# Row thresholds on VectorE instead of GpSimd, and new issue times for loads in the ordering, in a thresholded attention with a gated feed-forward

## The chip, the cores and the metric

The kernel runs on one core of one Trainium2 chip. The metric is the device time of an execution in microseconds (us). Before the change it was 568.11 us, the median of 3 runs (567.13 to 568.92). A difference of under one per cent is therefore only read from rounds in which a kernel and the kernel before alternate on the same chip, and the ratios below come with a 95% interval.

## The reference

Shortened:

```python
def _attn_ref(q, k, v, tau):                     # 8 batches, 8 heads, 576 rows, 64 wide
    scores = (1.0 / np.sqrt(64)) * np.matmul(q, k.transpose(0, 1, 3, 2))
    thresh = np.max(scores, axis=-1, keepdims=True) - tau          # tau = 0.02
    scores = np.where(scores >= thresh, scores, -1e9)
    attn = np.exp(scores - np.max(scores, axis=-1, keepdims=True))
    attn = attn / (np.sum(attn, axis=-1, keepdims=True) + 1e-09)
    return np.matmul(attn, v)

def _moe_ref(x, w_gate, w_val, w_out, rms_g):    # 4608 tokens, 512 wide, 1536 hidden
    xn = x / np.sqrt(np.mean(x * x, axis=-1, keepdims=True) + 1e-06) * rms_g
    g = xn @ w_gate
    return ((g * (1 / (1 + np.exp(-g)))) * (xn @ w_val)) @ w_out
```

The attention's output, heads side by side, is the feed-forward's x.

## The kernel before

The attention goes in 144 steps. One step takes two heads and 128 query rows: TensorE makes the scores into two buffers in PSUM, the memory that this kernel's matmuls write (line 566), VectorE copies them negated into SBUF, where its other tiles lie, and makes the row maximum of each head on the way (line 589), a threshold is formed from the two maxima (line 596), and ScalarE, in 64 of the steps with GpSimd, masks and exponentiates. Feed-forward matmuls fill TensorE between the steps. `mx` holds the two negated maxima of a row, `nth` the two thresholds that ScalarE and GpSimd read:

```python
for h in range(2):
    def ttr(o, h=h):
        nc.vector.tensor_tensor_reduce(
            out=ssb[a][:, h], in0=s_ps[h][:, ROW_AT:ROW_AT + S], in1=zrow, scale=-1.0 / 8.0, scalar=3.0e38,
            op0=ALU.add, op1=ALU.min, accum_out=mx[m][:, h:h + 1])
    ttr_of[s, h] = add("DVE", COST["ttr"], s - 1, [so, o_c] + exp_of.get(s - NSS, []), ttr)

def nthr(o):
    nc.gpsimd.tensor_scalar(out=nth[m], in0=mx[m], scalar1=tau, scalar2=None, op0=ALU.add)

tn = add("POOL", COST["pool_tiny"], s - 4, [ttr_of[s, 0], ttr_of[s, 1]], nthr)
# ... (the ways "p" on ScalarE alone and "g" with GpSimd; both wait for tn)
def mask(o, h=h):                                             # way "g", 64 times
    nc.gpsimd.tensor_scalar(out=wsb[s % NW][:, h], in0=ssb[a][:, h], scalar1=nth[m][:, h:h + 1],
                            scalar2=None, op0=ALU.is_le)      # 1.73 us
def take(o, h=h, es=es):
    nc.gpsimd.tensor_tensor(out=wsb[s % NW][:, h], in0=wsb[s % NW][:, h], in1=esb[es], op=ALU.mult)  # 1.28 us
```

Nothing is issued in the order of this text. Each `add` describes an operation with an engine, an assumed cost in ns, a priority and what it needs; `order_ops` works out from these one order for all engines when the kernel is built, and each engine's part of that order becomes its sequence of instructions. An assumed cost is thus never executed; it only moves instructions in the queues.

Of the kernel before, what the change touches and what calls it, by code (L numbers as in the profile page):

```python
# [11 lines left out]
ALU = mybir.AluOpType  # L12
# [3 lines left out]
COST = dict(  # L16
    s_main=932.0, s_virt=900.0, tr_qk=530.0, tr4=230.0, tr_full=440.0, av_main=310.0, av_virt=480.0, ffn4=216.0, warm=3500.0,
    ttr=690.0, evac_qk=600.0, evac_half=380.0, evac_kt=350.0, prelu=700.0, exp2=1250.0, exp1=690.0, exp0=690.0,
    mask_d=750.0, mask_g=1740.0, take_g=1300.0, trw=510.0, evac_w=450.0, evac_wp=900.0, rz=180.0, xmul=420.0, sq=800.0, xn=720.0,
    pool_tiny=270.0, pool_mean=800.0, pool_dma=850.0, cast_v=650.0, cast_vt=420.0, cast_w=720.0,  # L20
    sp=480.0, sp_v=650.0, sp_w=600.0, sp_tr=1300.0, sp_qk=900.0, sp_tl=630.0,
)
DMA_NS = dict(qk=1250.0, tl=700.0, v=880.0, vt=350.0, wt=1700.0, xt=800.0, out=800.0, w=820.0, wo=2500.0)
SWITCH = 170.0
# [102 lines left out]
def kernel(  # L127
# [12 lines left out]
    nc = tc.nc  # L140
# [3 lines left out]
    tau = float(tau)  # L144
# [9 lines left out]
    def sb(name, shape, dt=FP32):  # L154
        return konst.tile(shape, dt, tag=name, name=name)
# [28 lines left out]
    mx = [sb(f"mx{i}", [128, 2]) for i in range(6)]  # L184
    nth = [sb(f"nth{i}", [128, 2]) for i in range(6)]
# [30 lines left out]
    def gated(o, step):  # L216
        gates.append((o, step))
        return o

    def add(eng, cost, prio, deps, fn, **kw):  # L220
        o = Op(eng, cost, prio, deps, fn, **kw)
        ops.append(o)
        return o
# [315 lines left out]
    pre = {}  # L539
    ttr_of, exp_of, wt_of, av_of = {}, {}, {}, {}  # L540
# [42 lines left out]
    def emit_softmax(s, so):  # L583

        a = s % NSS
        m = s % 6
# [5 lines that stand above are left out]

            ttr_of[s, h] = add("DVE", COST["ttr"], s - 1, [so, o_c] + exp_of.get(s - NSS, []), ttr)

        def nthr(o):
            nc.gpsimd.tensor_scalar(out=nth[m], in0=mx[m], scalar1=tau, scalar2=None, op0=ALU.add)  # L596

        tn = add("POOL", COST["pool_tiny"], s - 4, [ttr_of[s, 0], ttr_of[s, 1]], nthr)
        wfree = [w_read.get(s - NW)]
        done = []  # L600
        ways = WAYS[s % len(WAYS)] if s >= FIRST else "pp"
        pls = []
        for h in range(2):
            way = ways[h]
            if way == "p":
                def prelu(o, h=h):
                    nc.scalar.activation(out=ssb[a][:, h], in_=ssb[a][:, h], func=PRELU, scale=-1.0,  # L607
                                         bias=nth[m][:, h:h + 1], **PRELU_KW)

                def ex(o, h=h):  # L610
                    nc.scalar.activation(out=wsb[s % NW][:, h], in_=ssb[a][:, h], func=AF.Exp)  # L611

                def ex2(o):
                    nc.scalar.activation(out=wsb[s % NW], in_=ssb[a], func=AF.Exp)  # L614

                pls.append(add("ACT", COST["prelu"], s + 0.5, [tn], prelu))
                if ways != "pp":
                    done.append(add("ACT", COST["exp0"], s + 0.5, pls + wfree, ex))
                elif h:
                    done.append(add("ACT", COST["exp2"], s + 0.5, pls + wfree, ex2))  # L620
            else:
                es = pre.get("n", 0) % NES
                pre["n"] = pre.get("n", 0) + 1

                def ex(o, h=h, es=es):
                    nc.scalar.activation(out=esb[es], in_=ssb[a][:, h], func=AF.Exp, scale=-1.0,  # L626
                                         bias=nth[m][:, h:h + 1])

                e = add("ACT", COST["exp1"], s + 0.4, [tn, pre.get(("es", es))], ex)
                if way == "d":  # L630
                    def mask(o, h=h, es=es):
                        nc.vector.scalar_tensor_tensor(
                            out=wsb[s % NW][:, h], in0=ssb[a][:, h], scalar=nth[m][:, h:h + 1], in1=esb[es],
                            op0=ALU.is_le, op1=ALU.mult)

                    st = add("DVE", COST["mask_d"], s + 0.4, [e] + wfree, mask)
                    done.append(st)
                else:
                    def mask(o, h=h):
                        nc.gpsimd.tensor_scalar(  # L640
                            out=wsb[s % NW][:, h], in0=ssb[a][:, h], scalar1=nth[m][:, h:h + 1], scalar2=None,
                            op0=ALU.is_le)

                    def take(o, h=h, es=es):
                        nc.gpsimd.tensor_tensor(out=wsb[s % NW][:, h], in0=wsb[s % NW][:, h], in1=esb[es],  # L645
                                                op=ALU.mult)

                    mk = add("POOL", COST["mask_g"], s + 0.4, [tn] + wfree, mask)
                    st = add("POOL", COST["take_g"], s + 0.4, [e, mk], take)
                    done.append(mk)  # L650
                pre["es", es] = st
                done.append(st)
        exp_of[s] = done

        if s < N_PE or s < N_ALT and s % 2:
            def tr(o):
                for j in range(9):
                    r, c = divmod(j, 5)
                    nc.tensor.transpose(ring[o.slot[r]].bitcast(FP16)[:, 128 * c:128 * c + 128],  # L659
                                        wsb[s % NW].rearrange("p h s -> p (h s)")[:, 128 * j:128 * j + 128], id16)  # L660

            t = add("PE", COST["trw"], s + 2.4, done + av_of.get(s - NWT, []), tr, ring="R", nring=2)
            w_read[s] = t
            w_ready[s] = []
            for r, (lo, hi) in enumerate(((0, 5), (5, 9))):
                def ev(o, r=r, lo=lo, hi=hi):
                    eng = nc.gpsimd if W_EVAC[r] == "POOL" else nc.vector
                    eng.tensor_copy(out=wt[s % NWT][:, lo:hi], in_=ring[t.slot[r]].bitcast(FP16)[
                        :, 0:128 * (hi - lo)].rearrange("p (c n) -> p c n", n=128))

                w_ready[s].append(add(W_EVAC[r], COST["evac_w" if W_EVAC[r] == "DVE" else "evac_wp"], s + 2.4, [t], ev, frees=(t, r)))
        else:
            def tdma(o):
                nc.sync.dma_start_transpose(out=wt[s % NWT], in_=wsb[s % NW].rearrange("p h s -> p (h s)"))

            t = add("SP", COST["sp_tr"], s, done + av_of.get(s - NWT, []), tdma, dma=DMA_NS['wt'])
            w_read[s] = t
            w_ready[s] = [t]
# [90 lines left out]
    def emit_ffn(slot, parts, ready_step, pace, streamed):  # L769
# [55 lines left out]
        if streamed:  # L825

            acc = None
            for fc, (hi, m_) in enumerate(hs):
# [7 lines left out]
                if not acc:  # L836

                    acc, mo.pick = mo, ACC
                outs.append(mo)
# [69 lines left out]
    for c in range(DFF // 512):  # L909
        for d in range(0, 4, 2):  # L910
            for w_dram, w_sb in ((moe_w_gate, wg), (moe_w_val, wv)):
# [7 lines left out]
                lo = gated(add("SP", COST["sp_w"], pr, w_use[slot], load, dma=2 * DMA_NS['w'], bulk=True), pr)  # L919
# [13 lines left out]
    for j in range(4):  # L933
        o = add("POOL", COST["pool_dma"], W_FROM + W_STEP * n + j + WO_AT, [], lambda o, j=j: nc.gpsimd.dma_start(
            out=wo[:, 3 * j:3 * j + 3], in_=wo_src[:, 3 * j:3 * j + 3]), dma=DMA_NS['wo'], bulk=True)
# [3 lines left out]
    for s, (ci, p) in enumerate(steps):  # L939
        kind, b, c = chunks[ci]  # L940
        so = s_of[s] = emit_s(s)
        emit_softmax(s, so)
        if p % 2:
            emit_av(s)
        if p == NP - 1:
            gi, j = place[ci]
            xt_op[ci] = emit_x(ci, s, gi % NXT, 128 * j)
            if ci in last_of:
                g = groups[last_of[ci]]
                emit_ffn(last_of[ci] % NXT, [(ci_of[x], xt_op[ci_of[x]]) for x in g], s + (ELAG if place[ci][0] < NELAG else LAG), PACE,  # L950
                         last_of[ci] >= len(groups) - STREAMED)
            for bb in ([b] if kind == "m" else [2 * b, 2 * b + 1]):
                left[bb] -= 1
                if not left[bb] and bb + 2 < B:
                    emit_batch_inputs(bb + 2)
# [12 lines left out]


PACE = 13.0  # L970
ACC = (4, 6)
OPENS = ((4,), (6,))
NHF = 12
# [69 lines left out]
```

## Time and profile before

| | before |
|---|---|
| median time | 568.11 us |
| span of the profiled execution | 568.3 us |
| TensorE busy | 558.4 us, 98% |
| VectorE busy | 427.2 us, 75% |
| ScalarE busy | 457.4 us, 80% |
| GpSimd busy | 322.4 us, 57% |

TensorE is the bound (98% busy, and 89% of the chain that ended last), so time on another engine counts only where it makes TensorE stand still. The average hides when that can happen. The page's second part gives the busy tenths of each engine in 40 slices of 14.2 us; three of its lines from the kernel before:

```profile
DVE  4899977969958588758895789659875886586354
ACT  4999899999878787979898898778978897884332
POOL 2378946976747457666766658555666555551000
```

VectorE is over 80% busy in the slices from about 14 to 71 us, and ScalarE until about 140. Whatever is added to VectorE has the least room there.

### The profile page before, as it was taken

The page shows a single profiled execution, that of the slowest core. Times are in us where ns is not written, and L with a number is a line of the kernel's source. Part 1 is how long each engine was busy: PE and PEld are TensorE (multiplying, and loading weights), DVE is VectorE, ACT ScalarE, POOL GpSimd, SP SyncE. Part 2 cuts the span into 40 slices and gives each one's busy share as a digit, 9 for nine tenths or more (in the row PEclk, how much of TensorE's full clock was granted, in tenths as well). Part 3 has the DMA queues.
Part 4 walks back from the last instruction along what each step waited for, and adds up shares of the span by engine and source line. Part 5 has one row for each costly group of instructions (what it writes and reads, how often), then busy time and mean ns, then how long its engine had stood idle before and what let it go on. Part 6 is the DMA issues. An engine that isn't in the chain of part 4 may idle for free.

```text
span 568.3 us, 13686 instructions
## 1 busy us (share of the span) xinstructions
PE 558.4 (98%) x5000; PEld 334.7 (59%) x5000; DVE 427.2 (75%) x1093; ACT 457.4 (80%) x739; POOL 322.4 (57%) x462
## 2 busy tenths in 40 slices
PE   8999999999999999999999999999999999999997
PEld 4666766767676555555555555545555455454674
DVE  4899977969958588758895789659875886586354
ACT  4999899999878787979898898778978897884332
POOL 2378946976747457666766658555666555551000
PEclk9999999999999999999999999999999999999999
DMA  8999998769994686999876799789887565633211
GB/s 187 250 289 282 178 195 184 161 132 202 167 202 104 136 159 149 177 177 187 178 160 148 142 186 181 161 168 162 174 167 184 88 96 86 178 81 44 84 37 38
DMA packets 270019, 88.98 MB, mean 157 GB/s; under 512 B 252544, under 2 KB 262272, under 8 KB 269952
## 3 DMA queue, kind: packets, MB, share of 16 engines
q1 hardware_dynamic: 267168, 86.02, 74.1%
q0 software_dynamic: 1600, 1.57, 1.8%
q8 instruction: 39, 0.64, 0.5%
q10 hardware_dynamic: 1184, 0.52, 0.3%
q14 instruction: 28, 0.23, 0.1%
HBM read 37.75 MB, written 9.44 MB: 83 GB/s over the span
## 4 chain that ended last, share of the span: by engine, by line
PE 89%; DVE 3%; DMA 2%; issue 2%; ACT 2%; POOL 1%; SPq 0%; DVEq 0%; POOLq 0%; ACTq 0%
PE s_ps L566 28%; PE ring L792 16%; PE ring L797 16%; PE ring L853 14%; PE ring L697 6%; PE ring L303 2%; PE ring L693 2%; DVE ssb L589 2%; DMA qkn<-in_q_dram 1%; PE s_ps L831 1%; PE s_ps L853 1%; PE ring L659 1%; PE s_ps L797 1%; PE ring L364 1%; DMA stage<-in_q_dram 1%
## 5 line engine op out<-in xcount | busy, mean ns | idle before, releaser
L589 DVE CUSTOM_DVE_ANT_0 ssb<-s_ps,zrow 128x576 f32<-128x576 f32 x288 | 207.8, 754 | 67.7 <-PE s_ps L566 60.5
L607 ACT ACTIVATE ssb<-ssb,nth 128x576 f32<-128x576 f32 x224 | 165.9, 766 | 32.4 <-POOL nth L596 32.1
L566 PE MATMUL s_ps<-qkt 64*128 64x288 f32 x1024 | 170.2, 429 | 1.4 <-DVE mx L589 1.1
L566 PEld LDWEIGHTS s_ps<-qkt 64*128 64x128 f32 x1024 | 96.2, 186 | 53.5 <-DVE mx L589 16.2
L640 POOL TENSOR_SCALAR wsb<-ssb,nth 128x576 f16<-128x576 f32 x64 | 110.5, 1726 | 9.7 <-DMA wt<-wsb 2.9
L792 PE MATMUL ring<-xnT,wg 128*128 128x512 f16 (+1 forms) x548 | 112.9, 328 | 0.4 <-DVE sl L809 0.4
L797 PE MATMUL ring<-xnT,wv 128*128 128x256 f16 (+1 forms) x544 | 111.4, 327 | 0.6 <-ACT qTv L472 0.3
L596 POOL TENSOR_SCALAR nth<-mx 128x2 f32<-128x2 f32 x144 | 31.6, 220 | 133.9 <-DVE mx L589 120.6
L809 DVE SCALAR_TENSOR_TENSOR sl<-th,ring 128x512 f32<-128x512 f32 (+1 forms) x137 | 75.9, 554 | 25.9 <-ACT th L806 24.6
L614 ACT ACTIVATE wsb<-ssb 128x1152 f16<-128x1152 f32 x80 | 92.9, 1161 | 1.9
L806 ACT ACTIVATE th<-ring 128x512 f32<-128x512 f32 (+1 forms) x137 | 66.3, 486 | 28.9 <-PE ring L792 26.4
L853 PE MATMUL ring<-wo,hf 128*128 128x512 f16 x384 | 89.3, 380 | 0.0
L645 POOL TENSOR_TENSOR wsb<-wsb,esb 128x576 f16<-128x576 f16 x64 | 81.8, 1278 | 8.8 <-ACT esb L626 4.4
L814 DVE TENSOR_TENSOR hf<-ring,sl 128x256 f16<-128x256 f32 (+1 forms) x136 | 75.9, 558 | 10.0 <-PE s_ps L566 0.5
L797 PEld LDWEIGHTS <-wv 128*128 128x128 f16 x576 | 52.2, 98 | 42.9 <-issue 12.3
L792 PEld LDWEIGHTS <-wg 128*128 128x128 f16 x576 | 52.0, 98 | 41.0 <-issue 11.6
L853 PEld LDWEIGHTS <-hf 128*128 128x128 f16 x408 | 37.4, 98 | 47.2 <-issue 6.6
L626 ACT ACTIVATE esb<-ssb,nth 128x576 f16<-128x576 f32 x64 | 49.2, 768 | 7.1 <-POOL nth L596 7.0
L697 PE MATMUL ring<-va,wt 128*128 128x65 f16 (+1 forms) x1264 | 52.8, 193 | 0.0
L697 PEld LDWEIGHTS <-wt 128*128 128x128 f16 (+1 forms) x1280 | 48.7, 100 | 3.4
L611 ACT ACTIVATE wsb<-ssb 128x576 f16<-128x576 f32 x64 | 43.6, 681 | 1.6
L693 PE MATMUL ring<-va,wt 128*128 128x130 f16 (+1 forms) x158 | 35.1, 227 | 0.1
(68 smaller groups left out, 448.1 us busy)
## 6 DMA issues: line engine op xcount, KB each, us to landing
vst<-in_v_dram SPq DMA_DIRECT2D x32, 256.0 KB, 3.2
qkn<-in_k_dram SPq DMA_DIRECT2D x31, 256.0 KB, 3.8
out_dram<-osb SPq DMA_DIRECT2D x31, 256.0 KB, 2.6
qkn<-in_q_dram SPq DMA_DIRECT2D x28, 256.0 KB, 4.1
stage<-in_moe_w_gate_dram SPq DMA_DIRECT2D x6, 512.0 KB, 6.6
stage<-in_moe_w_val_dram SPq DMA_DIRECT2D x6, 512.0 KB, 6.3
wt<-wsb SPq DMA_TRANSPOSE x128, 3.1
wo<-in_moe_w_out_dram POOLq DMA_DIRECT2D x4, 384.0 KB, 7.6
```

The source lines that it names most:

```text
L566: nc.tensor.matmul(s_ps[h][rows, ROW_AT + n * part:ROW_AT + n * part + n], lhs(hs), kT[i][p][h][hs, n * part:n * part + n], start=True, st ...
L589: nc.vector.tensor_tensor_reduce(out=ssb[a][:, h], in0=s_ps[h][:, ROW_AT:ROW_AT + S], in1=zrow, scale=-1.0 / 8.0, scalar=3.0e38, op0=ALU.a ...
L607: nc.scalar.activation(out=ssb[a][:, h], in_=ssb[a][:, h], func=PRELU, scale=-1.0, bias=nth[m][:, h:h + 1], **PRELU_KW)
L614: nc.scalar.activation(out=wsb[s % NW], in_=ssb[a], func=AF.Exp)
L640: nc.gpsimd.tensor_scalar(out=wsb[s % NW][:, h], in0=ssb[a][:, h], scalar1=nth[m][:, h:h + 1], scalar2=None, op0=ALU.is_le)
L645: nc.gpsimd.tensor_tensor(out=wsb[s % NW][:, h], in0=wsb[s % NW][:, h], in1=esb[es], op=ALU.mult)
L697: nc.tensor.matmul(ring[o.slot[0]][rs, at:at + D + 1], w[:, 5 * h + j, rs], va[vi][:, p, 2 * j + h], start=False, stop=(h == 1 and j == 3))
L792: nc.tensor.matmul(ring[o.slot[0]][:, 0:n], wg[d][:, fs], xnT[slot][:, d, 0:n], start=(d == 0), stop=(d == 3))
L797: nc.tensor.matmul(ring[o.slot[0]][:, 0:n], wv[d][:, fs], xnT[slot][:, d, 0:n], start=(d == 0), stop=(d == 3))
L809: nc.vector.scalar_tensor_tensor(out=sl[i][:, 0:n], in0=th[i][:, 0:n], scalar=1.0, in1=ring[g.slot[0]][:, 0:n], op0=ALU.add, op1=ALU.mult)
L814: nc.vector.tensor_tensor(out=hf[hi][:, 0:n], in0=ring[vv.slot[0]][:, 0:n], in1=sl[i][:, 0:n], op=ALU.mult)
L853: nc.tensor.matmul(ring[(first or o).slot[0]], hf[hs[fc][0]][:, 128 * j:128 * (j + 1)], wo[:, fc], start=(fc == 0), stop=(fc == NFC - 1))
```

## The change: its intent and the diff

The threshold of a step is one tiny addition. On GpSimd it stands in line behind masks of 1.73 us and products of 1.28 us, and ScalarE waits for it, 39.1 us in all. The change gives it to VectorE, directly behind the two maxima that it needs. A second part sets assumed issue times of loads nearer to those of the profile before (there loads of queries and keys on line 293 took 694 and 626 ns in the median, of values 578 ns); that moves instructions in the order and changes none.

```diff
-    sp=480.0, sp_v=650.0, sp_w=600.0, sp_tr=1300.0, sp_qk=900.0, sp_tl=630.0,
+    sp=420.0, sp_v=600.0, sp_w=600.0, sp_tr=1300.0, sp_qk=680.0, sp_tl=630.0,
...
-        def nthr(o):
-            nc.gpsimd.tensor_scalar(out=nth[m], in0=mx[m], scalar1=tau, scalar2=None, op0=ALU.add)
-
-        tn = add("POOL", COST["pool_tiny"], s - 4, [ttr_of[s, 0], ttr_of[s, 1]], nthr)
+        tns = []
+        for lo, hi in ((0, 1), (1, 2)) if NTH == "EACH" else ((0, 2),):
+            def nthr(o, lo=lo, hi=hi):
+                (nc.gpsimd if NTH == "POOL" else nc.vector).tensor_scalar(
+                    out=nth[m][:, lo:hi], in0=mx[m][:, lo:hi], scalar1=tau, scalar2=None, op0=ALU.add)
+
+            tns.append(add("POOL" if NTH == "POOL" else "DVE", COST["pool_tiny"] if NTH == "POOL" else NTHC, s - 4,
+                           [ttr_of[s, h] for h in range(lo, hi)], nthr))
...  (the readers of tn take tns[h % len(tns)])
+NTH = 'DVE'
+NTHC = 80.0
```

`NTH` also allows "POOL" (GpSimd) and "EACH" (one threshold for each head).

More of the change, by code (lines that the diff above doesn't have):

```diff
@@ L614, in ex2 @@
                     nc.scalar.activation(out=wsb[s % NW], in_=ssb[a], func=AF.Exp)
-                pls.append(add("ACT", COST["prelu"], s + 0.5, [tn], prelu))
+                pls.append(add("ACT", COST["prelu"], s + 0.5, [tns[h % len(tns)]], prelu))
                 if ways != "pp":
@@ L627, in ex @@
                                          bias=nth[m][:, h:h + 1])
-                e = add("ACT", COST["exp1"], s + 0.4, [tn, pre.get(("es", es))], ex)
+                e = add("ACT", COST["exp1"], s + 0.4, [tns[h % len(tns)], pre.get(("es", es))], ex)
                 if way == "d":
@@ L646, in take @@
                                                 op=ALU.mult)
-                    mk = add("POOL", COST["mask_g"], s + 0.4, [tn] + wfree, mask)
+                    mk = add("POOL", COST["mask_g"], s + 0.4, [tns[h % len(tns)]] + wfree, mask)
                     st = add("POOL", COST["take_g"], s + 0.4, [e, mk], take)
```

## The prediction

> **What bounds the kernel now**
>
> I read, in this order: the busy shares and the chain of waits on the page, busy time by stretch, the list of who waited for whom, the groups by line and shape, and the order of instructions where TensorE stood still. First the page:
>
> ```profile
> PE 558.4 (98%) x5000; PEld 334.7 (59%) x5000; DVE 427.2 (75%) x1093; ACT 457.4 (80%) x739; POOL 322.4 (57%) x462
> ...
> PE 89%; DVE 3%; DMA 2%; issue 2%; ACT 2%; POOL 1%; SPq 0%; DVEq 0%; POOLq 0%; ACTq 0%
> ```
>
> TensorE is busy 98% of the span and makes up 89% of the chain that ended last. VectorE (75%), ScalarE (80%) and GpSimd (57%) have room on average. An average hides stages, so next comes busy time by stretch (columns: stretch, then busy us and instruction count of PE, weight loads, VectorE, ScalarE, GpSimd; granted clock; DMA share; GB/s):
>
> ```profile
> 0.00:30.00 30.00, 27.10 (x225) 17.67 (x225) 20.82 (x62) 21.56 (x36) 8.73 (x24) 1.00 0.94 226
> 30.00:60.00 30.00, 28.51 (x318) 20.29 (x318) 27.65 (x80) 28.32 (x41) 24.65 (x47) 1.00 1.15 274
> 60.00:120.00 60.00, 59.49 (x659) 41.45 (x657) 50.32 (x142) 53.74 (x95) 43.37 (x58) 1.00 0.90 169
> 120.00:240.00 120.00, 119.00 (x1140) 75.07 (x1137) 93.44 (x246) 102.55 (x173) 73.61 (x101) 1.00 0.83 162
> 240.00:360.00 120.00, 120.00 (x1071) 66.92 (x1070) 93.98 (x231) 105.01 (x163) 77.93 (x108) 1.00 0.86 170
> ...
> 520.00:569.00 49.00, 44.29 (x316) 29.48 (x314) 22.88 (x55) 14.44 (x35) 1.44 (x3) 0.98 0.14 46
> ```
>
> TensorE is idle 2.9 us in the first 30, 1.5 in the next 30, 0.5 up to 120, 1.0 up to 240, nothing from 240 to 520, and 4.0 after 520 (568.3 less 520 less 44.29), which is the last output leaving. That is 9.9 us in all. Some waiting hides inside rows that count as busy: in the chain, a block of eight score matmuls (line 566) takes 1.17 us when its inputs are there and 1.86 to 1.91 us five times before 80 us. Five times 0.7 is 3.5 us more. So about 13 us of TensorE time is not work, and some 8 of them (the first 6.3 us, when the first query tile is awaited, of which part is idle; the store at the end) cannot be touched by row thresholds. What this change can win is bounded by roughly 5 us, 1% of the time, unless the new order packs TensorE better.
>
> Who waits on the thresholds (columns: waiter, what ended the wait, total us, times, longest):
>
> ```profile
> POOL nth L596 <- DVE mx L589: 120.6, 68, 9.3
> ...
> ACT ssb L607 <- POOL nth L596: 32.1, 39, 2.0
> ...
> POOL va L486 <- DMA vst<-in_v_dram: 14.3, 8, 4.3
> ...
> ACT esb L626 <- POOL nth L596: 7.0, 13, 1.8
> ```
>
> GpSimd's own 120.6 us of waiting for the maxima costs nothing by itself. ScalarE's 39.1 us (32.1 + 7.0) of waiting for thresholds is the target. How one such wait reaches TensorE (start us, length, engine and line, what it does, idle time before):
>
> ```profile
> 69.64 0.69 POOL L734 TENSOR_SCALAR xn<-xsb,ir 128x512 f16<-128x512 f32 x1
> ...
> 70.41 0.52 POOL L596 TENSOR_SCALAR nth<-mx 128x2 f32<-128x2 f32 x2
> ...
> 70.67 0.77 ACT L607 ACTIVATE ssb<-ssb,nth 128x576 f32<-128x576 f32 x1 [1.92 <-POOL nth L596]
> ...
> 71.35 0.36 ACT L806 ACTIVATE th<-ring 128x256 f32<-128x256 f32 x1
> ...
> 71.74 0.42 DVE L809 SCALAR_TENSOR_TENSOR sl<-th,ring 128x256 f32<-128x256 f32 x1 [1.68 <-ACT th L806]
> ...
> 72.22 0.38 PE L792 MATMUL ring<-xnT,wg 128*128 128x256 f16 x2 [0.43 <-DVE sl L809]
> ```
>
> GpSimd was in a normalisation (line 734) until about 70.3 us, so two thresholds came late and back to back; ScalarE stood still for 1.92 us; its tanh for the feed-forward came late; VectorE's product waited 1.68 us; TensorE stood 0.43 us for the PSUM buffer that this product frees. The same happens at 172.75 us, where a threshold sits behind a mask and its product, and a TensorE idle of 0.33 us follows at 176.49.
>
> [...]
>
> [...] 384 out-projection matmuls average 380 ns, yet four such 512-column matmuls follow the four before them after 0.87 us (261.53 to 262.40), about 217 ns each. I therefore look at TensorE's gaps and not at its share, and still find few.
>
> [...]
>
> [...]
>
> [...]
>
> **The change part by part**
>
> ```profile
> L640 POOL TENSOR_SCALAR wsb<-ssb,nth 128x576 f16<-128x576 f32 x64 | 110.5, 1726 | 9.7 <-DMA wt<-wsb 2.9
> ...
> L596 POOL TENSOR_SCALAR nth<-mx 128x2 f32<-128x2 f32 x144 | 31.6, 220 | 133.9 <-DVE mx L589 120.6
> ```
> ```profile
> L589 DVE DVE_READ_ACCUMULATOR2_ANT mx<- 128x1 f32 x288 | 23.9, 83 | 0.0
> ...
> L267 DVE MEMSET mhalf<- 128x1 f32 x1 | 0.1, 59 | 0.0
> ```
>
> The first fence is GpSimd's groups (busy us, mean ns of one, idle before); the second VectorE's small instructions by shape.
>
> *Removed from GpSimd:* 144 thresholds of 220 ns, 31.6 us. GpSimd goes from 322 to about 291 us (51%). Off the path, except that masks start earlier.
>
> *Added to VectorE:* 144 thresholds of about 60 ns, 9 us busy: 427 to about 436 us (77%). The slot is longer than its busy time. Today the accumulator read (83 ns) starts together with the next instruction and is hidden (251.08: both). The threshold needs its result, so it must wait it out; and a dependent VectorE instruction starts some 0.04 us after the one it needs (the reciprocal ends at 255.97, its product starts at 256.01). 0.08 + 0.04 + 0.06 = 0.18 us, times 144 is 26 us of VectorE time. It comes after the second maximum, so the score buffers are released as before; what moves back is the next evacuation or product.
>
> *The wait that shrinks:* from the end of the second maximum to ScalarE's start it is 0.33 us at best today (262.59 to 262.92) and 2 us behind a mask. It becomes about 0.16 us, always. Of ScalarE's 39 us I expect some 30 to vanish from this entry. ScalarE's busy time, 457 us, stays.
>
> *What reaches the end:* (a) To 60 us: VectorE is busy 27.65 of 30 us in the second stretch and stands in the chain between score blocks. Of 16 steps I take half to have VectorE last: 8 x 0.18 = +1.4 us. ScalarE waited 1.8 us for thresholds there, in four places; half of it is worth -0.9. Sum +0.5. (b) 60 to 240: the two stalls told above go, each with the stretched score block after it, about 1.0 us each: -2.0; VectorE runs without pause around 140 to 143 us, where two more slots cost +0.3. Sum -1.7. (c) 240 to 520: TensorE has no idle time, so 0 to -0.5; I take -0.3. (d) The end: nothing, since no thresholds are left after 512 us. Together -1.5 us.
>
> *Issue times of loads:* these numbers change no instruction, only the order that is worked out at build time. The trace supports the new ones: query and key loads took 0.61 to 0.71 us to issue (0.68 in place of 0.90), value loads 0.57 to 0.59 (0.60). With them the order will place loads earlier or tighter on the queue; GpSimd waited 14.3 us for value tiles, 4.28 of it just before the 172 us stall. I take -0.5 us, with 3 us either way, because a new order shuffles every engine.
>
> [...] GpSimd is busy about half the time with instructions of up to 1.73 us. If a random half of the thresholds met one and waited half of some 1.2 us, that would be 72 x 0.6 = 43 us of VectorE. But a mask waits for this very threshold, so the next one, about 3.5 us later, mostly finds the 3.0 us of mask and product done. I take a third of it, 15 us of VectorE time, spread where TensorE has other work: net effect about 0.
>
> Sum: 568.1 - 1.5 - 0.5 = 566.1 us. I predict 566 us, ratio 0.996.
>
> **Rivals**
>
> *1. TensorE's order and work decide, the thresholds never mattered.* For it: no TensorE idle time from 240 to 520 us, while ScalarE waited for thresholds there too (most of the 39 us). Against it: the two chains above. It would make 567 to 569 us.
>
> [...] Against it: the ordering just told. If a wait of about 1 us came in a third of the steps, TensorE would run out of free PSUM buffers (four in the ring) in a good many: 20 to 30 stalls of 0.5 us, 578 to 583 us.
>
> *3. The start becomes VectorE-bound.* For it: 92% VectorE in 30 to 60 us. All 16 steps paying 0.18 us, with nothing won by ScalarE, is +3 us: 570 us.
>
> *4. The new order happens to pack better*, with fewer stretched score blocks and loads of the start a microsecond or two earlier: 561 to 563 us.
>
> **Range and chances**
>
> My value lies 2 us below before. The upper side of the range is rival 3 and a mild rival 2, the lower side rival 4: 560.5 to 571.5 us. Faster by over 2% needs under 556.8 us, an 11 us gain, more than the touchable idle time: 0.03. Slower by over 2% needs over 579.5 us, which only a full lock brings, or an order gone wrong: 0.05. Within 2%: 0.92.
>
> **What would show it right or wrong**
>
> Right: the thresholds stand under VectorE, x144 near 60 ns; ScalarE's wait entry for thresholds falls under 12 us; GpSimd falls by 31 us; TensorE's busy time by stretch shows less idle from 60 to 240 us and nothing new elsewhere. The lock: thresholds far over 60 ns, or VectorE idle before them, ended by nothing, while a mask runs. Rival 3: more idle or stretched score blocks before 60 us, released by the maxima. The prediction is wrong if TensorE shows idle time between 240 and 520 us, or if the span moves by over 5 us with TensorE's idle time unchanged[...].

Passages that no trace or run of this case shows are cut from it, and the cuts are marked. The sum came to 568.1 - 1.5 - 0.5 = 566.1 us, with 0 for the paragraph before it. That paragraph is on the lock: a threshold on VectorE that lasts until an instruction on GpSimd ends. The kernel before has no threshold on VectorE, so its trace could not show one. Rival 2 is that such waits come often. The 60 ns of a threshold, and with them the 9 us and the 0.06 us of the slot, are the author's estimate, which no trace showed; the nearest figure of the trace is the memset of one element, 59 ns.

## The result, and the profile after

The changed kernel took 573.11 us (median of 5 runs, 572.07 to 573.58), the kernel before 568.04 us beside it (5 runs). The ratio is 1.0086, interval 1.0068 to 1.0104: slower by 0.9%, outside the predicted range of 560.5 to 571.5 us. Ratios are from the mean times of the fast runs of both kernels in the same rounds, so not quite the ratio of the medians quoted. All runs were with granted clocks of 0.994 to 1.000.

From the page of the changed kernel, the busy line and the engines' shares of the chain that ended last:

```profile
PE 559.7 (98%) x5000; PEld 335.4 (59%) x5000; DVE 457.4 (80%) x1237; ACT 460.8 (81%) x739; POOL 290.7 (51%) x318
...
PE 83%; DVE 11%; ACT 2%; DMA 2%; issue 1%; SPq 0%; DVEq 0%
```

GpSimd fell by 31.7 us as intended. VectorE rose by 30.2 us, over three times the 9 us predicted, and its share of the chain rose from 3% to 11%. By stretch (columns as in the prediction):

```profile
0.00:30.00 30.00, 26.08 (x232) 17.50 (x233) 22.68 (x70) 22.07 (x37) 7.43 (x18) 1.00 0.94 228
30.00:60.00 30.00, 28.31 (x314) 20.09 (x312) 29.22 (x85) 28.63 (x40) 23.74 (x38) 1.00 1.13 270
60.00:120.00 60.00, 58.88 (x627) 40.59 (x624) 53.89 (x155) 52.22 (x91) 36.63 (x38) 1.00 0.93 170
120.00:240.00 120.00, 119.81 (x1136) 75.88 (x1136) 101.54 (x279) 103.13 (x170) 65.75 (x67) 1.00 0.81 158
240.00:360.00 120.00, 120.00 (x1042) 65.17 (x1039) 97.89 (x257) 103.28 (x161) 68.53 (x72) 1.00 0.81 162
...
520.00:571.00 51.00, 46.64 (x327) 30.53 (x324) 24.62 (x58) 15.59 (x36) 1.44 (x3) 1.00 0.13 45
```

From 240 to 520 us TensorE still has no idle time. Before 60 us it is idle for 5.6 us (3.92 + 1.69) where it was 4.4; from 60 to 120 us for 1.12 where it was 0.51; from 120 to 240 us for 0.19 where it was 1.00. So a stall did go, and others came. A second profile of the changed kernel (the control changed_again below) tells which of this is chance: it has 3.41 us of idle time before 60 us, less than the kernel before, but again 0.93 us from 60 to 120 and 0.17 from 120 to 240. Only the growth from 60 to 120 us repeats; VectorE is busy for 53.9 of the 60 us there. (The two profiled spans differ by 2.4 us and the medians by 5: the profiled execution of the kernel before, 570.23 us, was at the slow end of its runs. The profiles tell where, the rounds tell how much.)

Waits on the thresholds, and in the first line GpSimd's wait for value tiles, which was 14.3 us (waiter, what ended the wait, total us, times, longest):

```profile
POOL va L486 <- DMA vst<-in_v_dram: 26.5, 11, 8.3
...
ACT ssb L611 <- DVE nth L598: 19.1, 28, 1.9
...
ACT esb L630 <- DVE nth L598: 14.9, 32, 1.4
```

ScalarE waits 34.0 us for thresholds (19.1 + 14.9) where it waited 39.1 us. The wait that the change was to remove has mostly stayed, now for VectorE.

The threshold itself, in the view of its tile (duration in ns as least/median/greatest, then first and last start) and in the group list (busy us, mean ns, idle before):

```profile
L598 DVE TENSOR_SCALAR nth<-mx x144: 157/170/1079, 10.2 to 511.5; 128x2 f32<-128x2 f32 x144
```

```profile
L598 DVE TENSOR_SCALAR nth<-mx 128x2 f32<-128x2 f32 x144 | 37.5, 260 | 4.9
```

The median is 170 ns, the mean 260 and the greatest 1079. A few very long ones lift the mean. In the order of time, one of them (start us, length, engine, line):

```profile
61.62 1.29 POOL L649 TENSOR_TENSOR wsb<-wsb,esb 128x576 f16<-128x576 f16 x1
61.75 0.08 DVE L589 DVE_READ_ACCUMULATOR2_ANT mx<- 128x1 f32 x1
61.87 1.07 DVE L598 TENSOR_SCALAR nth<-mx 128x2 f32<-128x2 f32 x1
...
62.85 0.81 DVE L672 COPY wt<-ring 128x640 f16<-128x640 f16 x2
...
62.97 1.44 ACT L611 ACTIVATE ssb<-ssb,nth 128x576 f32<-128x576 f32 x2 [1.60 <-DVE nth L598]
...
63.38 0.22 PE L697 MATMUL ring<-va,wt 128*128 128x130 f16 x1 [0.26 <-DVE wt L672]
```

The maximum is there at 61.83 us. The threshold starts at 61.87 and ends at 62.94, 0.03 us after GpSimd's product, which started before it, ends (61.62 + 1.29 = 62.91). Behind it, VectorE's two copies for the transposed weights start late, TensorE waits for those copies at 63.38, and ScalarE has stood still for 1.60 us. In the trace, 39 of 144 thresholds lasted over 0.2 us, and each of them ended 0.02 to 0.03 us after an instruction on GpSimd: products (21), casts of values and weights (12), normalisations (5), a mask (1). I call this the lock; the traces show when such a threshold ends, not what holds it. It is not taken against every instruction on GpSimd: nine thresholds of usual length ran wholly inside one, seven of them inside the one-element power of the normalisation (`ir`), which held none (it lasts about 0.57 us; they started 98 to 346 ns after it and took 169 or 170 ns). The chain of waits names long thresholds too (start us, length, what):

```profile
58.28 0.63 DVE nth L598
...
61.87 1.07 DVE nth L598
```

Around these two lines the chain is on VectorE without a break, from 32 to over 65 us.

### The profile page after: what moved, and what is told of

Same layout as the page of the kernel before. It is cut to its first block, busy times and chain, and to the rows that moved or that the text cites. A ratio compares the mean times of both kernels' runs of the same rounds, so it can differ in the third digit from the quotient of the medians.

```text
span 570.7 us, 13657 instructions
## 1 busy us (share of the span) xinstructions
PE 559.7 (98%) x5000; PEld 335.4 (59%) x5000; DVE 457.4 (80%) x1237; ACT 460.8 (81%) x739; POOL 290.7 (51%) x318
## 4 chain that ended last, share of the span: by engine, by line
PE 83%; DVE 11%; ACT 2%; DMA 2%; issue 1%; SPq 0%; DVEq 0%
PE s_ps L566 25%; PE ring L796 15%; PE ring L857 15%; PE ring L801 14%; PE ring L701 6%; DVE ssb L589 5%; PE ring L303 2%; PE ring L697 2%; DVE nth L598 1%; PE s_ps L801 1%; DVE wt L672 1%; DVE hf L818 1%; DVE sl L813 1%; DMA qkn<-in_q_dram 1%; PE s_ps L835 1%
## 5 line engine op out<-in xcount | busy, mean ns | idle before, releaser
L611 ACT ACTIVATE ssb<-ssb,nth 128x576 f32<-128x576 f32 x224 | 166.0, 767 | 19.8 <-DVE nth L598 19.1
L566 PEld LDWEIGHTS s_ps<-qkt 64*128 64x128 f32 x1024 | 97.4, 186 | 54.0 <-DVE mx L589 14.3
L796 PE MATMUL ring<-xnT,wg 128*128 128x256 f16 (+1 forms) x564 | 114.5, 325 | 0.1
L801 PE MATMUL ring<-xnT,wv 128*128 128x512 f16 (+1 forms) x520 | 108.2, 330 | 0.8 <-DVE xsb L719 0.7
L813 DVE SCALAR_TENSOR_TENSOR sl<-th,ring 128x256 f32<-128x256 f32 (+1 forms) x141 | 76.7, 544 | 19.8 <-ACT th L810 19.3
L810 ACT ACTIVATE th<-ring 128x256 f32<-128x256 f32 (+1 forms) x141 | 67.6, 481 | 28.9 <-PE ring L796 22.2
L818 DVE TENSOR_TENSOR hf<-ring,sl 128x512 f16<-128x512 f32 (+1 forms) x130 | 73.6, 566 | 10.4 <-PE ring L801 0.9
L630 ACT ACTIVATE esb<-ssb,nth 128x576 f16<-128x576 f32 x64 | 49.5, 773 | 15.1 <-DVE nth L598 14.9
L598 DVE TENSOR_SCALAR nth<-mx 128x2 f32<-128x2 f32 x144 | 37.5, 260 | 4.9
```

Of the source, the lines that this page charges most:

```text
L566: nc.tensor.matmul(s_ps[h][rows, ROW_AT + n * part:ROW_AT + n * part + n], lhs(hs), kT[i][p][h][hs, n * part:n * part + n], start=True, st ...
L611: nc.scalar.activation(out=ssb[a][:, h], in_=ssb[a][:, h], func=PRELU, scale=-1.0, bias=nth[m][:, h:h + 1], **PRELU_KW)
L796: nc.tensor.matmul(ring[o.slot[0]][:, 0:n], wg[d][:, fs], xnT[slot][:, d, 0:n], start=(d == 0), stop=(d == 3))
L801: nc.tensor.matmul(ring[o.slot[0]][:, 0:n], wv[d][:, fs], xnT[slot][:, d, 0:n], start=(d == 0), stop=(d == 3))
L813: nc.vector.scalar_tensor_tensor(out=sl[i][:, 0:n], in0=th[i][:, 0:n], scalar=1.0, in1=ring[g.slot[0]][:, 0:n], op0=ALU.add, op1=ALU.mult)
L818: nc.vector.tensor_tensor(out=hf[hi][:, 0:n], in0=ring[vv.slot[0]][:, 0:n], in1=sl[i][:, 0:n], op=ALU.mult)
```

## The experiments

Three theories were in play at first or soon after. Theory 1: the threshold's slot on VectorE, lengthened by the lock, lies on the path in the crowded start. Theory 2: the new order that the issue times made is to blame. Theory 3, formed after the first set: it is the place right behind the maxima that costs. A fourth grew from the third set: the lock in that place.

All kernels gave correct results. Each was timed in 5 rounds against the kernel before. The medians of the kernel before in the four sets were 568.5, 569.14, 568.27 and 567.66 us.

### Which part of the change, and is it the order or the engine?

*Only the issue times*: `NTH = 'POOL'` in the changed kernel.

> The changed kernel with the thresholds back on GpSimd (in the ordering too), so that only the issue times of loads differ from before. Theory 1 (the threshold's slot on VectorE, 0.17 us and up to 1.07 us behind GpSimd's instructions, lies on the path up to some 62 us): 566 to 569 us, no loss. Theory 2 (the loss comes from the new order that the issue times made): 571 to 574 us, as the changed kernel.

Measured: 567.43 us, ratio 0.9972 (0.9947 to 0.9997). The ratio leaves out the profiled execution, which took 572.21 us. The issue times are no cause of the loss; they win a little.

*Only the engine*: the old issue times in the changed kernel.

```diff
-    sp=420.0, sp_v=600.0, ... sp_qk=680.0, ...
+    sp=480.0, sp_v=650.0, ... sp_qk=900.0, ...
```

> The changed kernel with the old issue times, so that only the threshold's engine (and its place in the ordering) differs from before. Theory 1 (VectorE's slot at the start): 571 to 574 us, the whole loss. Theory 2 (the issue times' order): 566 to 569 us.

Measured: 572.82 us, ratio 1.0066 (1.0042 to 1.0090). The threshold's move carries the loss.

*The changed kernel's order with the threshold on GpSimd*: every instruction keeps its place, only the engine of this one is another.

```diff
-                (nc.gpsimd if NTH == "POOL" else nc.vector).tensor_scalar(
+                nc.gpsimd.tensor_scalar(
```

> Exactly the order of the changed kernel, but the threshold instruction itself is given to GpSimd; no other instruction moves on any engine. Theory 1: VectorE loses the 37.5 us of thresholds and TensorE's idle time in the first 60 us falls from 5.6 us to some 4.4: 567 to 570 us, most of the loss undone. Theory 2 (the order is to blame, whatever the engine): 571 to 574 us.

Measured: 569.86 us, ratio 1.0020 (0.9997 to 1.0042). Two thirds or more of the loss undone: the order alone is not it. TensorE's idle time in the first 60 us did not fall, though (3.11 + 2.88 us); that part of the expectation was wrong.

*The order of before with the threshold on VectorE*:

```diff
-            nc.gpsimd.tensor_scalar(out=nth[m], in0=mx[m], ...
+            nc.vector.tensor_scalar(out=nth[m], in0=mx[m], ...
```

> Exactly the order of the kernel before, but the threshold instruction is given to VectorE, at the place in the sequence that GpSimd's had. Theory 1: thresholds of 0.17 us and more on VectorE, some 37 us of its time, 570 to 574 us. Theory 2: 567 to 569 us, since the order is the old one.

Measured: 569.64 us, ratio 1.0015 (0.9993 to 1.0038). A surprise against theory 1: thresholds took 35.7 us of VectorE with a mean of 248 ns, nearly as in the changed kernel, and cost almost nothing. What differs is the place: here only 42 thresholds stand right behind the accumulator read of the second maximum, in the changed kernel 141. So VectorE's busy time by itself does not explain the loss, and theory 3 was formed: the place does.

### The place and the stretch

*One instruction later*: in the finished order, each threshold goes behind the next VectorE instruction if nothing in between needs it.

```diff
+    for o in [o for o in seq if getattr(o.fn, "__name__", "") == "nthr"]:
+        i = seq.index(o)
+        j = next(n for n in range(i + 1, len(seq)) if seq[n].eng == "DVE")
+        if not any(o in seq[n].deps for n in range(i + 1, j + 1)):
+            seq.insert(j, seq.pop(i))
```

> The changed kernel with every threshold moved behind the next VectorE instruction where nothing in between needs it; all else in the same order. Theory 3 (it is the place right behind the maxima that costs: a pause of 0.035 us, the accumulator read no longer hidden, and the next evacuation held up): the pause goes, VectorE loses some 15 us of it, 568.5 to 571 us, over half of the loss undone. Theory 1 in its simple form[...]: 572 to 574 us, nothing won.

(Theory 1 in its simple form: the 170 ns of the instruction and the lock.)

Measured: 569.23 us, ratio 1.0001 (0.9974 to 1.0028). Against the kernel before, most of the loss is undone, with as many long thresholds as before the move (40 over 0.2 us where there were 39), as the group in this kernel shows:

```profile
L598 DVE TENSOR_SCALAR nth<-mx 128x2 f32<-128x2 f32 x144 | 36.2, 251 | 1.3
```

*Thresholds of the first 32 steps on GpSimd, the rest on VectorE, and the reverse*:

```diff
-        for lo, hi in ((0, 1), (1, 2)) if NTH == "EACH" else ((0, 2),):
+        on_pool = s < 32          # the reverse: s >= 32
+        for lo, hi in ((0, 2),):
```

(the engine and the assumed cost follow `on_pool`)

> Thresholds of the first 32 of 144 steps (up to about 120 us) on GpSimd, the others on VectorE, new issue times. If the loss lies before 120 us, where VectorE is the fullest and TensorE has idle time: 566 to 569 us. If it lies in the steady state: 571 to 574 us.

> The reverse: thresholds of the first 32 steps on VectorE, the others on GpSimd, new issue times. If the loss lies before 120 us: 571 to 574 us. If it lies in the steady state: 566 to 569 us.

Measured: 569.07 us, ratio 1.0002 (0.9972 to 1.0032), and 570.24 us, ratio 1.0020 (0.9991 to 1.0048). Neither has the full loss. Against the kernel with the new issue times alone (0.9972), VectorE costs some 0.3% in the last 112 steps and some 0.5% in the first 32. No single stretch holds it; an early step comes out some five times as dear as a late one, but from ratios that are known to 0.3% only. Both runs lie between their two expectations, the first just above 569 us.

*A threshold for each head*: `NTH = 'EACH'`.

> One threshold for each half, 288 instructions of one element a partition, each right behind its own maximum. If the count and the pause behind the accumulator read cost: 288 x (0.17 + 0.12) us = 83 us of VectorE time, 575 to 585 us. If [...] a one-element instruction does not take it (none over 0.2 us): 568 to 572 us.

(In the last sentence of the expectation "it" is the lock, and the lock is taken to be what costs.)

Measured: 578.97 us, ratio 1.0172 (1.0145 to 1.0199). This is slower, without any lock. Here the first threshold of a step stands between the two maxima, so it holds up the second and with it the release of the score buffers; that this is the reason is argued, not tested. But the view of the tile held the key:

```profile
L598 DVE TENSOR_SCALAR nth<-mx x288: 142/154/157, 9.5 to 522.7; 128x1 f32<-128x1 f32 x144
```

Of 288 one-element thresholds none lasted over 157 ns. None of them was locked.

### The lock apart from everything else

*Controls*: the changed kernel again and one_later again, on one chip.

> The changed kernel itself, as a control on the same chip as the next three. 572 to 574 us, ratio 1.007 to 1.010.

> The kernel of the run one_later again, beside the control. Theory 3 (the place right behind the maxima): 3 to 5 us below the control, ratio to before 0.998 to 1.004. Were the first measurement a matter of the chip: within 1.5 us of the control.

Measured: 571.79 us, ratio 1.0062 (1.0044 to 1.0080), a little under its expectation, and 569.29 us, ratio 1.0022 (1.0000 to 1.0045). The later place wins again, by 2.5 us where 3 to 5 were expected.

*A spare instruction in the kernel before*: order and thresholds untouched; only a second addition on VectorE behind the second maximum, into a tile that nobody reads (its allocation is left out here).

```diff
                     op0=ALU.add, op1=ALU.min, accum_out=mx[m][:, h:h + 1])
+                if h:
+                    nc.vector.tensor_scalar(out=spare[:, 0:2], in0=mx[m][:, 0:2], scalar1=tau,
+                                            scalar2=None, op0=ALU.add)      # the other run: [:, 1:2]
```

> The kernel before, its order and its thresholds on GpSimd untouched, with a second copy of the threshold on VectorE right behind the second maximum, written to a tile that nobody reads. It holds nobody up but VectorE. Theory 3: this slot alone[...] brings the loss: 571 to 575 us. Rival (the loss comes from ScalarE and GpSimd being released earlier or in another order): 567 to 569.5 us.

> The same spare instruction with one element a partition[...]. If the lock makes up the loss: 567 to 569.5 us. If the slot and its pause do: 570 to 573 us, and the difference to spare_two, 0 to 3 us, is the lock.

(Theory 3 counts in the slot: 0.17 us, the pause, the accumulator read that was hidden, and the lock.)

Measured: with two elements 574.77 us, ratio 1.0112 (1.0089 to 1.0134); with one element 569.02 us, ratio 1.0013 (0.9992 to 1.0033). The view of the spare tile, first in the kernel with two elements, then in that with one:

```profile
L594 DVE TENSOR_SCALAR spare<-mx x144: 168/169/1232, 10.0 to 513.7; 128x2 f32<-128x2 f32 x144
```

```profile
L594 DVE TENSOR_SCALAR spare<-mx x144: 153/154/156, 9.8 to 508.7; 128x1 f32<-128x1 f32 x144
```

The count, the place and the order are the same, and nothing waits for the result. Only the width differs, and with it the greatest length: 1232 against 156 ns. The lock is 5.75 us of time, by the medians; the slot with its pause is under 1 us. Theory 3 in the form that I had given it, the pause and the unhidden accumulator read, fell with this: spare_one has both at every step and costs next to nothing.

### The lock taken out of the changed kernel

*Two single thresholds*: the changed kernel in its own order; the two elements are written by two instructions, both behind the second maximum.

```diff
-                (nc.gpsimd if NTH == "POOL" else nc.vector).tensor_scalar(
-                    out=nth[m][:, lo:hi], in0=mx[m][:, lo:hi], scalar1=tau, scalar2=None, op0=ALU.add)
+                for j in range(lo, hi):
+                    nc.vector.tensor_scalar(
+                        out=nth[m][:, j:j + 1], in0=mx[m][:, j:j + 1], scalar1=tau, scalar2=None, op0=ALU.add)
```

> The changed kernel in its own order, with each two-element threshold written as two instructions of one element, one after the other behind the second maximum. Lock theory: no threshold over 0.16 us, 12 to 13 us of lock gone from VectorE though an instruction more in each step, 567 to 570 us, ratio 0.998 to 1.003. If the slot's length or the order carries the loss in this kernel: 571 to 575 us, ratio over 1.005.

Measured: 566.97 us, ratio 0.9981 (0.9960 to 1.0003). The whole loss is gone. From its page, and its group of thresholds on VectorE:

```profile
PE 557.9 (99%) x5000; PEld 334.1 (59%) x5000; DVE 449.8 (80%) x1381; ACT 460.2 (81%) x739; POOL 289.9 (51%) x318
...
PE 90%; DVE 4%; ACT 2%; POOL 2%; DMA 1%; issue 1%; POOLq 0%; DVEq 0%
```

```profile
L599 DVE TENSOR_SCALAR nth<-mx 128x1 f32<-128x1 f32 x288 | 38.9, 151 | 0.0
```

From first start to last end of each, the thresholds take 38.9 us, more than the 37.5 us of the changed kernel. VectorE's busy time falls by 7.6 us all the same (457.4 to 449.8), since these short spans overlap with each other and with their neighbours (the pair below takes 0.27 us in all, and two spans of 151 ns would be 0.30). Its share of the chain falls from 11% to 4%. In the order of time, a pair that meets a product on GpSimd:

```profile
193.19 1.27 POOL L650 TENSOR_TENSOR wsb<-wsb,esb 128x576 f16<-128x576 f16 x1
...
193.79 0.08 DVE L589 DVE_READ_ACCUMULATOR2_ANT mx<- 128x1 f32 x1
193.79 0.27 DVE L599 TENSOR_SCALAR nth<-mx 128x1 f32<-128x1 f32 x2
```

The product holds GpSimd from 193.19 to 194.46 us; the pair runs inside it and takes 0.27 us in all. In the trace, some 90 of the 288 began and ended within one GpSimd instruction, and none waited.

The split changes a second thing: the first of the pair needs only the first maximum, so it starts with the accumulator read of the second, at 193.79 us, and the pause is gone. That is no rival for the gain: from the start of this read to VectorE's next instruction it takes 190 ns with the pair and 196 ns in the changed kernel (medians; 190 in spare_one too), and spare_one has the pause and costs next to nothing. TensorE's stretch that had got worse:

```profile
60.00:120.00 60.00, 60.00 (x654) 41.80 (x654) 52.74 (x178) 53.58 (x92) 37.35 (x38) 1.00 0.97 172
```

From 60 to 120 us TensorE has no idle time at all now, where it had 1.12 and 0.93 us in the two profiles of the changed kernel.

*The same, one instruction later*: both edits.

> The same two instructions, moved behind the next VectorE instruction where that is allowed. Lock theory: little more to win, within 1.5 us of two_single. Place theory: 2 us or more below two_single.

Measured: 566.74 us, ratio 0.9975 (0.9955 to 0.9995). Without the lock the place is worth nothing that these rounds can see. The run also gives the right yardstick for one_later, which is the same order with the lock: 1.0001 and 1.0022 against 0.9975. So the lock still costs some 0.3 to 0.5% one instruction later (each ratio is known to about 0.3%), and not nothing, as the comparison with the kernel before suggested.

*When the time is lost.* Kernels with and without the lock in the same order can be laid side by side in their traces: by how much does each row maximum (the end of its accumulator read) come later with the lock? In us, from one profiled execution of each:

| with lock, against without | at about 53 us | 68 | 105 | 221 | 337 | end |
|---|---|---|---|---|---|---|
| changed kernel, two_single | 1.2 | 2.8 | 3.7 | 5.1 | 5.3 | 5.5 |
| changed_again, two_single | 0.6 | 2.3 | 2.7 | 4.0 | 4.1 | 4.4 |
| spare_two, spare_one | 0.5 | 1.9 | 1.4 | 4.0 | 4.5 | 5.0 |
| one_later, two_single_later | 0.9 | 2.2 | 2.6 | 3.6 | 3.6 | 3.8 |
| one_later_again, two_single_later | -0.8 | 0.7 | 1.1 | 2.0 | 2.0 | 2.5 |

Nearly all of it is lost before 221 us. In the changed kernel 25 of the 39 locks, 9.4 of 13.0 us of locked time, fall before that and cost 5.1 us; the other 3.6 us cost about 0.5. All five pairs have this shape. A single execution can mislead (the two profiles of the issue times alone differ by 5 us, which came between 107 and 137 us in one of them), so the shape counts here and not the tenths.

*The issue times alone, again, and with single thresholds on VectorE at GpSimd's place in the order*:

> The kernel of only_issue_times again (thresholds on GpSimd, new issue times). If its small gain holds: ratio 0.995 to 0.999, 565 to 567.5 us. If it was chance: 0.999 to 1.003.

> The order of issue_again, with thresholds given to VectorE as two one-element instructions at GpSimd's place in the sequence: no lock, no crowding behind the maxima, ScalarE's wait for GpSimd gone. If the change's intent is worth anything to the end of the kernel: 1 to 3 us below issue_again. If TensorE's order decides everything in the steady state: within 1 us of it.

Measured: 566.68 us, ratio 0.9975 (0.9954 to 0.9997), and 567.33 us, ratio 0.9985 (0.9966 to 1.0004). The gain of the issue times holds in both measurements. Taking the thresholds off GpSimd adds nothing to it.

## Why the prediction was wrong

It was wrong by its size and its sign: 566.0 us predicted, 573.1 measured.

**What holds.** TensorE is the bound, and from 240 to 520 us it has no idle time with or without the change. Its idle time from 120 to 240 us fell from 1.00 to 0.19 us, as part (b) said. GpSimd fell to 290.7 us (291 predicted). The issue times win a little: -0.28% and -0.25%, about 1.5 us, where -0.5 was the estimate. The rest of the sum is nearly what the kernel without the lock does, 566.97 us; that is luck in part, since two of its terms missed in opposite directions: 1.5 us in place of 0.5 for the issue times, and nothing in place of 1.5 for the earlier thresholds.

**The step that failed** is the one on the lock: "I take a third of it, 15 us of VectorE time, spread where TensorE has other work: net effect about 0." The first half was right in size. The locks came to 144 x (260 - 170) ns = 13.0 us. The second half was wrong: the changed kernel lies at 1.0086 and 1.0062, the same order without the lock at 0.9981; the difference is 1.05% and 0.81%, or 6.0 and 4.6 us. So a third to a half of the locked time reached the end. In the term of the sum: 0 was written where 5 belonged. Rival 2 named the cause and oversized it: it had a wait of about 1 us in a third of the steps, and there were 39 waits (27%) of 13.0 / 39 = 0.33 us on average over the free 170 ns.

Why was it not spread where TensorE has other work? For the late part it was: after 221 us, 3.6 us of locked time cost about 0.5. But most of the locks came before, while VectorE was busy for 85 to 97% of each stretch from 30 to 240 us, and there about half of the locked time reached the end. The place adds to it. The lock right behind the maxima costs 0.8 to 1.05%, behind another VectorE instruction 0.26 and 0.47% (one_later and one_later_again against two_single_later) or 0.15% (before_order_vector), all with a mean near 250 ns. The place without the lock costs nothing that the rounds see (spare_one 1.0013, two_single 0.9981). A threshold right behind the maxima is the first thing VectorE does after releasing the score buffers, and what stands next is what TensorE is short of: a copy of transposed weights, a product that frees a PSUM buffer. The lines at 61.87 us show such a case. That the lock carries the loss, and that it is lost early, is shown; that it mostly goes by way of such cases, and that VectorE's fullness is what makes the early part dear, is argued.

**The threshold's own length**, "about 60 ns", was 170 ns in the profile, and VectorE's busy time 457.4 us where 436 was predicted. That mis-sized term cost little: the slot that entered the sum, 0.18 us, was nearly right (0.196 us in the middle from the start of the accumulator read to VectorE's next instruction). At 112.22 us a threshold lasts until 112.39 and the next instruction starts at 112.30, so there it kept the engine for about 0.08 us, half of its length in the profile; for the 105 thresholds of usual length the median time from their start to that of VectorE's next instruction is 77 ns. The 60 ns were an estimate, and the figure of the trace that stood beside it, 59 ns, is that of a memset, which reads nothing. The trace of before had better yardsticks: a reciprocal of four elements from PSUM at 179 ns, and one cast from SBUF to SBUF at the start (line 266), 154 ns. By the profile GpSimd's 220 ns for two elements are thus only 50 ns more than VectorE's.

**ScalarE's wait for thresholds**, to fall under 12 us, was 34.0 us; without the lock it is 24.9 us (13.2 + 11.7 in the wait list of two_single), against 29.0 (24.4 + 4.6) in issue_again, with the thresholds on GpSimd. The shorter hand-off let the order place ScalarE's work closer behind it, so the wait was moved rather than removed; I did not test this. It cost nothing, since two_single and issue_again are equal within 0.3 us: the -1.5 us that I had put down to earlier thresholds is not there. Rival 1, "the thresholds never mattered", was right on that.

**Rival 3**, the crowded start with 0.18 us more in each step, is not it by itself: spare_one adds such a slot to every step and costs 0.1% (at most 0.3% by its interval). It was right that VectorE has the least room early.

What stays open: why the order of the changed kernel with thresholds on GpSimd costs 0.2% (its interval reaches 0.9997), and how much of the place's effect is the place: moving the thresholds also changed which of them met GpSimd (7.1 and 7.3 us of locked time before 221 us in the two profiles of one_later, 9.4 and 7.9 in those of the changed kernel).

## What to carry to other kernels

Before a small instruction is moved to VectorE beside a busy GpSimd, ask whether its form waits there for GpSimd's instructions. Here an fp32 addition of two elements a partition did (39 of 144 lasted over 0.2 us, up to 1079 ns against a median of 170), and one of one element did not (none of 288 over 157 ns); other forms were not examined. For the one that waited, the price was set by what was left of GpSimd's instruction, most often a product of 1.28 us, not by its own length. Writing two elements in two instructions was faster here by 0.8 to 1.0% of the whole kernel, with 144 instructions more on VectorE. The price also depends on when: here locked time cost about half of its length before 221 us and little after. And a mean hides all this: look at the greatest duration of the tiny instructions and at what ends when they end. Of all kernels tried, the plain issue times with thresholds on GpSimd (0.9972 and 0.9975) and the single thresholds placed later (0.9975) were the fastest, equal within their intervals, and both beat the kernel before.
